# Scalar steps on VectorE, normalising in gated slots on GpSimd, and sums in need order, in a fused attention and GLU kernel

## The chip, the cores and the metric

The kernel runs on one core of a Trainium2 chip. The metric is device time in microseconds (us) of one execution; medians over several executions are quoted. Each execution also has a *span*, the time from the first to the last instruction in the trace, which is some 1.7 us shorter. Five engines work side by side (in the profile before PE is busy for 97% of the span, DVE for 81%), each with its own program: PE (TensorE, matmuls), DVE (VectorE), ACT (ScalarE), POOL (GpSimd) and SP (SyncE, which issues DMAs). The traces show DVE and POOL keeping to the order of their programs. In the kernel before, the inputs of a one-element product on POOL were ready by 102.81 us, but behind the steps in front of it in the program it ran only at 109.00 us. DVE stood idle for 3.94 us for its result, and a sum behind that wait, to whose input ACT had nothing left to add after 105.81 us, started only at 109.31 us.

## The reference

The sum of an input, a linear attention with a learned feature map, and a bilinear GLU, both on the layer norm of the input (2048 tokens, width 512, 32 heads of 16, inner width 1792, bf16):

```python
xn = _layernorm(x)
# attention: q, k, v = heads of xn @ wqkv
phi(q) = concat(softmax(q @ w_phi), softmax(-q @ w_phi)); phi(k) likewise
kv = einsum("bhsf,bhsd->bhfd", phi_k, v);  z = sum of phi_k over s
o  = einsum("bhqf,bhfd->bhqd", phi_q, kv) / (einsum("bhqf,bhf->bhq", phi_q, z) + 1e-6)
A  = o @ wo
# GLU
h = (xn @ w_gate) * (xn @ w_up);  B = h @ w_down
return x + A + B
```

## The kernel before

A list scheduler at build time orders the steps on each engine. Matmuls keep the program's order. The tokens are 16 tiles of 128. In *slot* t of the main loop PE computes k features and v of some tile, two to four GLU units (`up`), and from slot 10 on one or two q features.

- A GLU unit is two groups of matmuls into two PSUM banks; ACT copies one out, and DVE multiplies the other with it (line 817, "the gate product" below). There are two pairs of banks, so PE can start the second group of a unit only when the gate product of two units earlier is done.
- A feature tile goes through ACT (two exponentials), DVE (a sum, line 512), ACT (a reciprocal by logarithm and exponential), POOL (lines 520 and 522, scaling one half). A q tile is then transposed by a DMA.

The end of the kernel multiplies h in fp16, with w_down scaled by a power of two (line 699, after the scale is known) and combined by a Strassen-like scheme (`wd_combine`, line 748; sums of h, line 778). Tiles 0 to 3 were computed before their layer norm was known, so their h must be multiplied by a row `r2`: 14 products on POOL (line 727). The parts that the change touches:

```python
    def norms(lo, n, k):                       # line 670
        ...
        pool(lambda e: e.tensor_copy(out=ssqb[:, lo:lo + n], in_=ssq[:, lo:lo + n]), cols, [("ssqb", lo)], n)
        ...                                    # a matmul, a DVE sum, two ACT steps
    def d_scale():                             # line 690, slot 12
        norms(14, 7, 1)
        power_of_two(swd, scl[:, 18:19], [("rn", 14)], "swd", 4096.0)           # DVE, lines 665, 666
        pool(lambda e: e.tensor_tensor(out=scl[:, 22:23], in0=sh, in1=swd, op=ALU.mult), ["sh", "swd"], ["both"], 1)  # line 693
        dve(lambda e: e.reciprocal(out=scl[:, 23:24], in_=scl[:, 22:23]), ["both"], ["rboth"], 1)                      # line 694
        ...
    def normalise(fts):                        # line 724, called in slots 13 to 16
        sc.prio = 2
        for ft in fts:
            pool(lambda e, ft=ft: e.tensor_tensor(out=hH_v[:, ft, 0:512], in0=hT_v[:, ft, 0:512], in1=r2w,
                                                  op=ALU.mult), [("hT", ft, 0), "r2w", ("x", 14), ("x", 15)],
                 [("hT", ft, 0)], 512)
    # ... cut
    for t in range(NT + 3):                    # the slots
        features("ek", t, 1)                   # ... cut: k features, then units, v, q features
```

The scheduler places the products of `normalise` by its own model of time: in the order it built, they start soon after slot 11 and stand between the features on POOL.

The softmax here doesn't subtract the row's maximum and nothing guards it: scores larger than these inputs give would overflow.

## Time and profile before

| | |
|---|---|
| median time | 221.18 us (3 runs, 220.29 to 221.28) |
| span of the profiled run | 219.1 us |
| busy: PE, DVE, ACT, POOL | 97%, 81%, 58%, 39% |

PE is the limit nearly everywhere, so the question is where it waits. From the page of the profile, the shares of busy time and the rows of 40 slices of 5.5 us (each digit is the busy share in tenths; PEclk is the clock granted to PE):

```profile
PE 211.5 (97%) x1472; PEld 127.2 (58%) x1492; DVE 176.9 (81%) x293; ACT 126.2 (58%) x316; POOL 84.4 (39%) x151
...
PE   7899999999999999999979999999999999999995
...
POOL 3032543424023205508999988040313414330220
PEclk9999999999999999999969999999999999999999
```

One slice stands out, the 21st (109.6 to 115.0 us): PE is at 7 and its clock at 6, and POOL is full around it. The stretches around it show both (columns: stretch, its length, then busy time of PE, weight loads, DVE, ACT, POOL, then granted clock, DMA share and GB/s):

```profile
105.00:109.00 4.00, 4.00 (x20) 1.68 (x18) 0.29 (x1) 0.58 (x3) 4.00 (x6) 1.00 0.10 18
109.00:111.10 2.10, 0.18 (x1) 0.00 (x0) 1.87 (x5) 0.53 (x3) 2.10 (x4) 1.00 0.00 0
111.10:114.70 3.60, 3.54 (x12) 1.36 (x13) 3.60 (x9) 2.12 (x4) 3.60 (x7) 0.53 0.42 81
114.70:120.00 5.30, 5.25 (x31) 2.48 (x30) 5.30 (x8) 3.60 (x10) 5.14 (x7) 1.00 0.29 56
120.00:130.00 10.00, 9.84 (x52) 4.48 (x52) 9.97 (x11) 6.51 (x16) 8.76 (x10) 1.00 0.25 49
```

DVE and ACT stand nearly still from 105 to 109 us, while POOL is full; then PE stands still; then PE works at half clock; and from 111 to 130 us DVE has no idle time left. The timeline shows why (start, length, engine, line; in brackets the idle time before and what ended it):

```profile
104.08 1.21 DVE L512 TENSOR_REDUCE arena<-arena 128x64 f32<-128x1024 bf16 x1
...
105.42 3.40 POOL L727 TENSOR_TENSOR arena<-arena 128x512 f16<-128x512 bf16 x3
108.77 0.27 POOL L520 TENSOR_TENSOR arena<-arena 128x32 f32<-128x32 f32 x1
109.00 0.20 POOL L693 TENSOR_TENSOR arena<-arena 128x1 f32<-128x1 f32 x1
...
109.23 0.16 DVE L694 RECIPROCAL arena<-arena 128x1 f32<-128x1 f32 x1 [3.94 <-POOL arena L693]
109.31 1.20 DVE L512 TENSOR_REDUCE arena<-arena 128x64 f32<-128x1024 bf16 x1
...
110.42 0.68 DVE L817 TENSOR_TENSOR arena<-ps,arena 128x512 f16<-128x512 f32 x1
...
111.16 1.39 PE L244 MATMUL ps<-arena 128*128 128x512 bf16 x3 [1.98 <-DVE arena L665]
```

The one-element product of line 693 stands on POOL behind normalising products. DVE, in its program's order, waits 3.94 us for it, and behind DVE's wait stands the gate product (110.42 us) that PE needs. (PE's wait is put down to line 665, a tiny step that ended at 111.16 us, 0.06 us after the gate product; no matmul reads its result.)

### The profile page before, as it was taken

Reading aid. Unit: us, or ns where it says so; the run is one execution under the profiler, and the core shown is the slowest. Engines: PE = TensorE matmul, PEld = TensorE weight load, DVE = VectorE, ACT = ScalarE, POOL = GpSimd, SP = SyncE. Lnnn points to the kernel's source line nnn. Section 1 sums busy time; section 2 is a strip of 40 time slices with the busy share of each in tenths; the row PEclk is TensorE's granted clock in tenths of the full one; section 3 lists DMA queues with packets and bytes.
Section 4 is the critical chain, followed back from the end, with each engine's and each line's share of the span. In section 5 each row is a group of like instructions: output and inputs, shape, how many; then the busy total and the mean of one; then the engine's idle time right before and its main releaser. Section 6 shows DMA issues by size and latency. Waiting matters only on the chain.

```text
span 219.1 us, 4039 instructions
## 1 busy us (share of the span) xinstructions
PE 211.5 (97%) x1472; PEld 127.2 (58%) x1492; DVE 176.9 (81%) x293; ACT 126.2 (58%) x316; POOL 84.4 (39%) x151
## 2 busy tenths in 40 slices
PE   7899999999999999999979999999999999999995
PEld 2474444444444454444324444455988889899984
DVE  3848999997699898777299998988999999785332
ACT  5558899878778636767256586644343542622330
POOL 3032543424023205508999988040313414330220
PEclk9999999999999999999969999999999999999999
DMA  5999790079400000021233322546053494654431
GB/s 169 288 297 372 182 136 0 15 209 306 99 0 0 0 0 3 0 61 39 49 68 60 65 48 51 96 126 114 2 138 72 130 121 112 158 123 123 104 88 48
DMA packets 49076, 22.30 MB, mean 102 GB/s; under 512 B 38048, under 2 KB 47392, under 8 KB 49056
## 3 DMA queue, kind: packets, MB, share of 16 engines
q1 hardware_dynamic: 48112, 21.39, 41.8%
q10 hardware_dynamic: 944, 0.66, 1.0%
q8 instruction: 11, 0.18, 0.3%
q14 instruction: 9, 0.07, 0.1%
HBM read 11.03 MB, written 2.10 MB: 60 GB/s over the span
## 4 chain that ended last, share of the span: by engine, by line
PE 78%; DVE 6%; issue 5%; POOL 5%; DMA 3%; ACT 1%; SPq 0%; POOLq 0%
PE ps L244 74%; POOL arena L727 3%; DMA arena<-in_A_wqkv_dram 3%; DVE arena L512 3%; PE ps L619 2%; DVE arena L699 2%; DVE arena L817 1%; PE ps L562 1%; POOL arena L522 1%; ACT arena L225 1%; PE ps L374 1%; POOL arena L520 1%; DVE arena L550 0%; SPq L269 0%; DVE arena L842 0%
## 5 line engine op out<-in xcount | busy, mean ns | idle before, releaser
L244 PE MATMUL ps<-arena 128*128 128x512 bf16 (+2 forms) x1156 | 201.6, 330 | 3.8 <-DVE arena L665 2.0
L244 PEld LDWEIGHTS ps<-arena 128*128 128x128 bf16 (+1 forms) x1176 | 112.4, 98 | 78.8 <-DVE arena L665 2.5
L225 ACT ACTIVATE arena<-ps 128x512 bf16<-128x512 f32 (+4 forms) x107 | 53.3, 530 | 37.6 <-PE ps L619 16.5
L225 ACT ACTIVATE arena<-arena 128x32 f32<-128x32 f32 (+7 forms) x117 | 38.8, 345 | 21.3 <-DVE arena L512 18.1
L512 DVE TENSOR_REDUCE arena<-arena 128x64 f32<-128x1024 bf16 x32 | 38.7, 1213 | 8.2 <-ACT arena L225 8.0
L817 DVE TENSOR_TENSOR arena<-ps,arena 128x512 bf16<-128x512 f32 (+1 forms) x56 | 38.0, 683 | 8.2 <-ACT arena L225 4.5
L225 ACT ACTIVATE arena<-ps,arena 128x512 bf16<-128x512 f32 (+1 forms) x49 | 31.0, 653 | 12.2 <-PE ps L244 12.1
L522 POOL TENSOR_TENSOR arena<-arena 128x512 bf16<-128x512 bf16 x32 | 34.5, 1080 | 1.1
L520 POOL TENSOR_TENSOR arena<-arena 128x32 f32<-128x32 f32 x32 | 9.3, 292 | 52.5 <-DVE arena L817 29.6
L862 POOL TENSOR_TENSOR arena<-arena 128x256 f32<-128x256 f32 x16 | 11.0, 711 | 45.6 <-ACT arena L225 45.6
L842 DVE SCALAR_TENSOR_TENSOR arena<-ps,arena 128x256 bf16<-128x256 f32 x32 | 14.9, 479 | 12.1 <-PE ps L244 11.9
L778 DVE TENSOR_TENSOR arena<-arena 128x896 f16<-128x896 f16 x32 | 22.1, 715 | 0.0
L727 POOL TENSOR_TENSOR arena<-arena 128x512 f16<-128x512 bf16 x14 | 17.4, 1255 | 6.7 <-DMA arena<-r2row 6.7
L225 ACT ACTIVATE ps<-ps 128x256 f32<-128x256 f32 x24 | 8.8, 368 | 16.0 <-PE ps L244 15.7
L629 DVE TENSOR_TENSOR arena<-ps,arena 128x512 bf16<-128x512 f32 x16 | 10.9, 685 | 1.6 <-ACT arena L225 1.6
L654 DVE SCALAR_TENSOR_TENSOR arena<-arena 128x1024 bf16<-128x1024 bf16 x7 | 11.9, 1721 | 0.0
L401 DVE BATCH_NORM_STATS2 arena<-arena 128x6 f32<-128x512 bf16 x16 | 10.5, 671 | 0.1
L550 DVE TENSOR_TENSOR arena<-ps,arena 128x512 bf16<-128x512 f32 x14 | 9.5, 682 | 0.0
L562 PEld LDWEIGHTS ps<-arena 128*128 128x128 bf16 x128 | 6.2, 99 | 3.9 <-issue 0.6
L459 POOL TENSOR_SCALAR arena<-arena 128x1 f32<-128x1 f32 x12 | 3.3, 302 | 12.0 <-ACT arena L225 12.0
L562 PE MATMUL ps<-arena 128*128 128x68 bf16 x128 | 6.6, 195 | 0.0
L619 PE MATMUL ps<-arena 128*128 128x68 bf16 x128 | 6.5, 194 | 0.0
(52 smaller groups left out, 72.2 us busy)
## 6 DMA issues: line engine op xcount, KB each, us to landing
arena<-in_A_x_dram SPq DMA_DIRECT2D x9, 256.0 KB, 3.1
out_dram<-arena SPq DMA_DIRECT2D x15, 128.0 KB, 2.0
arena<-in_B_w_down_dram SPq DMA_DIRECT2D x1, 1792.0 KB, 8.2
arena<-in_A_x_dram SPq DMA_DIRECT2D x3, 512.0 KB, 4.2
arena<-arena SPq DMA_TRANSPOSE x44, 3.1
arena<-in_B_w_gate_dram SPq DMA_DIRECT2D x1, 640.0 KB, 8.5
arena<-in_B_w_up_dram SPq DMA_DIRECT2D x1, 640.0 KB, 9.7
arena<-in_B_w_gate_dram SPq DMA_DIRECT2D x1, 512.0 KB, 5.1
```

Of the source, the lines that this page charges most:

```text
L225: return sc.step(ACT, lambda e: e.activation(out=out_ap, in_=in_ap, func=func, scale=scale, **kw), reads, writes, 130.0 + 0.833 * n)
L244: ins = e.matmul(out_ap, lhsT=l, rhs=r, start=start and i == 0, stop=stop and i == npair - 1, **kw)
L512: dve(lambda e: e.tensor_reduce(out=sm, in_=e_v, axis=AX.X, op=ALU.add), [(name, s, 0), (name, s, 1)], [("sums", sr)], 1024)
L520: pool(lambda e: e.tensor_tensor(out=rat, in0=sm[:, :, 0], in1=rs[:, :, 1], op=ALU.mult), [("sums", sr), ("rs", n)], [("rat", n)], 32)
L522: pool(lambda e: e.tensor_tensor(out=e_v[:, :, 1, :], in0=e_v[:, :, 1, :], in1=rat[:, :, None].to_broadcast([128, H, 16]), op=ALU.mult), [ ...
L562: ins = e.matmul(bank(c // 4, (c % 4) * CW, CW), lhsT=ek[:, c * 128:(c + 1) * 128], rhs=vs[:, c * CW:(c + 1) * CW], start=(t == 0 and c % ...
L654: dve(lambda e: e.scalar_tensor_tensor(out=junk, in0=i_ap, scalar=1.0, in1=i_ap, op0=ALU.mult, op1=ALU.mult, accum_out=ssq[:, col:col + 1] ...
L727: pool(lambda e, ft=ft: e.tensor_tensor(out=hH_v[:, ft, 0:512], in0=hT_v[:, ft, 0:512], in1=r2w, op=ALU.mult), [("hT", ft, 0), "r2w", ("x" ...
L778: dve(lambda e, k=k, i0=i0, i1=i1, op=op: e.tensor_tensor(out=s_block(p, k), in0=i0, in1=i1, op=op), ks + more, [s_key(p, k)] + over.get(k ...
L817: dve(lambda e: e.tensor_tensor(out=h_v[:, ft, sg * 512:(sg + 1) * 512], in0=bank(bu), in1=g, op=ALU.mult), [("ps", bu), ("g", s)] + ([("j ...
L842: dve(lambda e: e.scalar_tensor_tensor(out=stg, in0=bank(b, 0, 256), scalar=inv, in1=resid, op0=ALU.mult, op1=ALU.add), [("ps", b), rkey, ...
L862: pool(lambda e, h=h: e.tensor_tensor(out=xs[h], in0=s7, in1=xr_tile(t1)[:, h * 256:(h + 1) * 256], op=ALU.add), ["s7", ("xr", t1 % 4)], [ ...
```

## The change

Its intent: take POOL out of the chain of scale steps; have POOL normalise h of tiles 0 to 3 in slots 11 to 15, three units a slot, each group only after the slot's latest GLU unit is gated, so that the products keep to their slots; and compute the sums of a pair in the order in which the products at the end need them. The diff, cut to its core:

```diff
     def norms(lo, n, k):
-        pool(lambda e: e.tensor_copy(out=ssqb[:, lo:lo + n], ...
+        dve(lambda e: e.tensor_copy(out=ssqb[:, lo:lo + n], ...
     def h_scale():
-        pool(lambda e: e.tensor_tensor(out=scl[:, 20:21], in0=scl[:, 12:13], in1=scl[:, 13:14], op=ALU.mult),
+        dve(lambda e: e.tensor_tensor(out=scl[:, 20:21], in0=scl[:, 12:13], in1=scl[:, 13:14], op=ALU.mult),
     def d_scale():
-        pool(lambda e: e.tensor_tensor(out=scl[:, 22:23], in0=sh, in1=swd, op=ALU.mult), ["sh", "swd"], ["both"], 1)
+        dve(lambda e: e.tensor_tensor(out=scl[:, 22:23], in0=sh, in1=swd, op=ALU.mult), ["sh", "swd"], ["both"], 1)
...          (r2w moves from the space of x tiles 14, 15 to that of 12, 13)
-    def normalise(fts):
+    def normalise(fts, after):
-                   op=ALU.mult), [("hT", ft, 0), "r2w", ("x", 14), ("x", 15)],
+                   op=ALU.mult), [("hT", ft, 0), "r2w", ("x", 12), ("x", 13)] + after,
...          (h_combine: the order of its sums)
-        sc.prio = 2
+        sc.prio = 2 if p else 1
         for k, i0, i1, op, more in ((1, a21, a22, ALU.add, []),
+                                    (3, a11, a21, ALU.subtract, [s_key(p, 1)]),
                                     (2, s_block(p, 1), a11, ALU.subtract, [s_key(p, 1)]),
-                                    (3, a11, a21, ALU.subtract, [s_key(p, 1)]),
                                     (4, a12, s_block(p, 2), ALU.subtract, [s_key(p, 2)])):
...          (row_of_r2 is called in slot 10 instead of 11)
-        if 13 <= t < 17:
-            normalise(range(14 * (t - 13) // 4, 14 * (t - 12) // 4))
+            if 11 <= t < NT:
+                normalise(range(14 * (t - 11) // 5, 14 * (t - 10) // 5), [("hT", *latest[0])])
```

More of the change, by code (lines that the diff above doesn't have):

```diff
@@ L672, in norms @@
         cols = [("ssq", c) for c in range(lo, lo + n)]
-        pool(lambda e: e.tensor_copy(out=ssqb[:, lo:lo + n], in_=ssq[:, lo:lo + n]), cols, [("ssqb", lo)], n)
+        dve(lambda e: e.tensor_copy(out=ssqb[:, lo:lo + n], in_=ssq[:, lo:lo + n]), cols, [("ssqb", lo)], n)
         b = misc_bank()
@@ L719, in row_of_r2 @@
         sc.dma(SP, lambda e: e.dma_start(o, r2s, allow_slow_non_contiguous=True), ["r2s"], ["r2row"], 131072)
-        ks = [("x", 14), ("x", 15)]
+        ks = [("x", 12), ("x", 13)]
         wide = bass.AP(tensor=row.tensor, offset=row.offset, ap=[[0, 128], [1, ND * 128]])
         sc.dma(SP, lambda e: e.dma_start(r2w, wide), ["r2row"], ["r2w"] + ks, 262144, free=ks)
-    def normalise(fts):
+    def normalise(fts, after):
         sc.prio = 2
@@ L732, in _build @@
     r2s = scl[:, 4:4 + ND]
-    r2w = sbf("x", 3584, 512)
+    r2w = sbf("x", 3072, 512)
     tw = {k: sbh(f"tw{k}", 0, NK * 256).rearrange("p (f j) -> p f j", f=NK) for k in (1, 2, 3, 4)}
@@ L978, in scales @@
             h_scale()
+            row_of_r2()
         if 7 <= t < 11:
@@ L981, in scales @@
                 squares("wd", i, last)
-        if t == 11:
-            row_of_r2()
-        elif t == 12:
+        if t == 12:
             d_scale()
```

## The prediction

> **What bounds the kernel now.** TensorE. The page has PE busy 211.5 of 219.1 us (97%), DVE 81%, ACT 58%, POOL 39%. In the stretch table PE is busy in 9.84 to 10.00 us of nearly every 10 us from 20 to 210 us, except around 110 us. In the list of waits PE waited on an engine only once for over 1 us: 1.98 us, from 109.18 to 111.16 us. Right after it (111.1 to 114.7 us) the granted clock is 0.53, and 8 matmuls of 512 columns took 3.52 us, where others take about 0.22 each. The clock record holds half speed for 3.41 us: about 1.7 us more is lost. [...] The stall costs 2.0 + 1.7 = 3.7 us.
>
> **Why PE waits.** The chain of waits runs POOL, DVE, PE. GpSimd waits 6.73 us for the row of r2 (to 99.1 us), then works without a pause: six normalising products (1.1 to 1.2 us each), features, and only at 109.0 us the one-element product of the scales (line 693). DVE, in order, waits 3.94 us for it before the reciprocal (109.23 us). Behind that stand a 1.2 us sum and the gate product that frees the PSUM bank PE wants (ends 111.10 us).
>
> **What the change does.**
> 1. Scalar steps on VectorE: four more DVE instructions of about 0.15 us (the like of lines 665, 666, 694), 0.6 us in all, and the 3.94 us wait gone. Counting from 102.8 us with the trace's durations, the gate product that ended at 111.10 us should end near 107.5, 1.5 us before PE wants its bank; later gates come early enough too. This is the whole gain. The first scale's product and the two copies gain nothing: nothing on PE waited for them.
> 2. Normalising in slots 11 to 15, three per slot: GpSimd's sum is unchanged (14 products, 17.4 us), spread to about 138 us instead of 133.6. Not on PE's path: this h is wanted near 146 us (142 after). The row of r2 keeps its place in the DMA queue, so GpSimd still waits some 6 us for it. Worth 0.
> 3. Sums of the first pair in need order: PE shows no wait from 146 to 160 us. Worth 0.
>
> **Predicted.** 221.18 - 3.7 + 0.1 for added DVE work = 217.6 us, 1.6% faster. Range 216.7 to 219.6. Chances: faster by over 2% 0.06, within 2% 0.92, slower by over 2% 0.02.
>
> **What would show it.** Step 1: no DVE wait at the reciprocal, PE's 2 us wait gone, granted clock 1.00 from 100 to 125 us, about 0.22 us per 512-column matmul there. Step 2: last normalising product near 135 to 140 us; the first sum of the pair doesn't wait for POOL. Step 3: no PE wait in the first output pair. Span near 215.5 us.
>
> **What would make it wrong.** VectorE was full (9.97 of 10 us from 120 to 130 us); with PE earlier, a gate may come late there[...], leaving a gain of 1 to 2 us. GpSimd, in order, may wait for a gated unit and hold features back. The last normalising products may come late for the first sum and stall the start of the outputs. Or the clock drop has a cause other than the wait.

Two passages are cut where marked: one on what brings the half clock, one on how long a wait brings it; no trace of this case shows either. 221.18 - 3.7 + 0.1 = 217.6 us (217.58), with 3.7 = 2.0 (PE's wait of 1.98 us) + 1.7 (3.41 us at half clock), both read from the trace. The "gain of 1 to 2 us" in its last paragraph was the estimate for a half clock that comes back.

## More of the kernel before

The q tiles use a ring of three buffers, so ACT's exponentials of a q tile wait until the DMA has read the tile three before.

- v is computed into a PSUM bank and scaled by DVE (line 550). k, v and q features share two PSUM banks.

## The result

The changed kernel takes 217.51 us (median of 4 runs, 217.38 to 217.83), the kernel before 221.07 us (4 runs, 220.29 to 221.28). The ratio is 0.9847, with a 95% interval of 0.982 to 0.9874. Here and below a ratio is the mean time of one kernel's fast runs over that of the other's in the same rounds, so it is not quite the ratio of the medians. On another occasion the changed kernel took 218.44 us beside 221.80 us, ratio 0.9841 (0.9817 to 0.9865).

The profile after. The page's rows:

```profile
PE 210.7 (97%) x1492; PEld 126.6 (59%) x1492; DVE 178.0 (82%) x297; ACT 126.3 (58%) x316; POOL 82.8 (38%) x147
...
PE   7999999999999999999999979999999999999995
...
POOL 3032453423122023405999699720322413420220
PEclk9999999999999999999999999999999999999999
```

The dip at the 21st slice is gone and the clock is full throughout; a new, smaller dip of PE stands at the 24th (124 to 130 us). The same stretches as before:

```profile
105.00:109.00 4.00, 4.00 (x20) 1.81 (x19) 3.78 (x6) 2.29 (x7) 3.84 (x7) 1.00 0.61 67
109.00:111.10 2.10, 2.10 (x18) 1.11 (x17) 2.10 (x4) 1.17 (x3) 2.10 (x3) 1.00 0.37 68
111.10:114.70 3.60, 3.60 (x19) 1.60 (x18) 3.60 (x5) 2.87 (x9) 3.52 (x5) 1.00 0.48 75
114.70:120.00 5.30, 5.30 (x33) 2.58 (x32) 5.21 (x7) 3.23 (x8) 5.22 (x8) 1.00 0.27 53
120.00:130.00 10.00, 8.90 (x49) 4.00 (x48) 9.62 (x10) 5.83 (x15) 8.21 (x11) 1.00 0.27 52
```

PE now has no idle time until 120 us, and loses 1.10 us in the next 10. The timeline:

```profile
102.65 0.54 DVE L693 TENSOR_TENSOR arena<-arena 128x1 f32<-128x1 f32 x1
...
103.22 0.16 DVE L694 RECIPROCAL arena<-arena 128x1 f32<-128x1 f32 x1
...
105.80 0.68 DVE L817 TENSOR_TENSOR arena<-ps,arena 128x512 f16<-128x512 f32 x1
...
118.48 1.38 DVE L699 TENSOR_SCALAR arena<-arena 128x1024 f16<-128x1024 bf16 x1
...
119.90 1.94 DVE L748 TENSOR_TENSOR arena<-arena 128x1792 f16<-128x1792 f16 x1
...
123.48 1.14 DVE L748 TENSOR_TENSOR arena<-arena 128x1792 f16<-128x1792 f16 x1
...
128.00 0.68 DVE L550 TENSOR_TENSOR arena<-ps,arena 128x512 bf16<-128x512 f32 x1
...
128.73 1.04 PE L244 MATMUL ps<-arena 128*128 128x512 bf16 x4 [1.10 <-DVE arena L550]
```

The reciprocal comes 6 us earlier, without a wait, and the gate product that PE wanted at 109 us ends at 106.5 us. The new wait is for the scaling of v (line 550), which frees a PSUM bank: DVE reaches it late, because it has been busy without a pause and has just combined w_down twice (line 748).

A measure that serves for all runs below: the time on PE from its first state sums (line 562, near 102 us) to its first output heads (line 619, near 145 to 150 us). PE's work in between is the same in every kernel here. It took 46.47 us before and 43.63 us after; the fastest profile of all had 42.36 us. Against that fastest profile PE lost about 4.1 us there before and 1.3 us after. Of the difference of 2.84 us, the wait of 1.98 and the half clock (3.41 us of half speed, so 1.71) went, and 1.10 came: 2.59. The remaining 0.25 us are small gaps that I do not assign.

### The profile page after: what moved, and what is told of

Same layout as the page of the kernel before. It is cut to its first block, busy times and chain, and to the rows that moved or that the text cites. A ratio compares the mean times of both kernels' runs of the same rounds, so it can differ in the third digit from the quotient of the medians.

```text
span 216.1 us, 4056 instructions
## 1 busy us (share of the span) xinstructions
PE 210.7 (97%) x1492; PEld 126.6 (59%) x1492; DVE 178.0 (82%) x297; ACT 126.3 (58%) x316; POOL 82.8 (38%) x147
## 4 chain that ended last, share of the span: by engine, by line
PE 91%; DMA 3%; DVE 3%; issue 1%; ACTq 0%; ACT 0%; DVEq 0%
PE ps L244 86%; DMA arena<-in_B_w_gate_dram 3%; PE ps L619 2%; PE ps L562 2%; DVE arena L512 1%; DVE arena L817 1%; PE ps L374 1%; DVE arena L748 0%; DVE arena L550 0%; DVE arena L842 0%; ACTq L289 0%; ACT L1074 0%; PE ps L480 0%; DVEq L1175 0%
## 5 line engine op out<-in xcount | busy, mean ns | idle before, releaser
L522 POOL TENSOR_TENSOR arena<-arena 128x512 bf16<-128x512 bf16 x32 | 35.4, 1108 | 1.3
L520 POOL TENSOR_TENSOR arena<-arena 128x32 f32<-128x32 f32 x32 | 8.7, 271 | 47.9 <-DVE arena L817 30.5
L778 DVE TENSOR_TENSOR arena<-arena 128x896 f16<-128x896 f16 x32 | 22.7, 727 | 0.1
L461 DVE TENSOR_SCALAR arena<-arena 128x512 bf16<-128x512 bf16 x12 | 5.3, 484 | 1.7 <-DMA arena<-arena 1.4
L619 PE MATMUL ps<-arena 128*128 128x68 bf16 x128 | 6.5, 194 | 0.0
```

The lines of the kernel that those rows point to most:

```text
L522: pool(lambda e: e.tensor_tensor(out=e_v[:, :, 1, :], in0=e_v[:, :, 1, :], in1=rat[:, :, None].to_broadcast([128, H, 16]), op=ALU.mult), [ ...
L619: ins = e.matmul(bank(b0 + c // 4, (c % 4) * CW, CW), lhsT=ph[:, c, :], rhs=kvz_v[:, c, :], start=True, stop=True)
L778: dve(lambda e, k=k, i0=i0, i1=i1, op=op: e.tensor_tensor(out=s_block(p, k), in0=i0, in1=i1, op=op), ks + more, [s_key(p, k)] + over.get(k ...
```

## The experiments

### First call: which part gives the gain

Four kernels on one chip, with 11 runs of the kernel before (median 221.17 us). `s1_only` and `line693_only` start from the kernel before:

```diff
  s1_only: all three lines of step 1 as in the change (two helpers and line 693: pool -> dve)
  line693_only:
-        pool(lambda e: e.tensor_tensor(out=scl[:, 22:23], in0=sh, in1=swd, ...
+        dve(lambda e: e.tensor_tensor(out=scl[:, 22:23], in0=sh, in1=swd, ...
  s2_only: the change with these three lines back on pool, and without step 3
  no_s3: the change without its edit of h_combine
```

> The kernel before with step 1 alone (all three kinds of scalar steps on VectorE). My theory: step 1 by itself takes away DVE's 3.94 us wait and with it PE's 1.98 us wait and the half-rate window, so the time is that of the full change, 217.5 us within 0.4, clock 1.00 from 100 to 125 us. Rival: the full change also needs the moved normalising to be fast; then this run keeps part of the stall and lies at 218.5 to 220.

Measured: 219.77 us (219.45 to 219.89), ratio 0.993 (0.9915 to 0.9944). So step 1 alone gives 1.4 us, not 3.5: my theory fell, and the rival's range of 218.5 to 220 holds it. DVE's wait of 3.94 us and PE's of 1.98 us are gone as expected, and the clock is full; but PE has a new wait. The timeline of this kernel:

```profile
105.62 3.41 POOL L727 TENSOR_TENSOR arena<-arena 128x512 f16<-128x512 bf16 x3
...
109.52 1.11 POOL L522 TENSOR_TENSOR arena<-arena 128x512 bf16<-128x512 bf16 x1
...
114.10 0.60 ACT L225 ACTIVATE arena<-ps 128x512 bf16<-128x512 f32 x1 [4.20 <-DMA arena<-arena]
...
115.36 0.82 PE L244 MATMUL ps<-arena 128*128 128x512 bf16 x3 [1.73 <-ACT arena L225]
```

and its chain of waits:

```profile
105.67 3.36 POOL arena L727 x3
109.04 0.41 POOL arena L520
...
109.52 1.12 POOL arena L522
...
110.70 3.04 DMA arena<-arena
...
114.10 1.21 ACT arena L225 x3
```

Three normalising products (3.4 us) stand on POOL in front of the scaling of a q tile. The q tile's transposition by DMA starts only after that (3.04 us), and ACT, which wants the buffer of that q tile for a new one, waits 4.20 us. Behind ACT, in order, stands what PE needs. This is the path that step 2 is about, and that the prediction left out.

> The kernel before with only the product of the two scales (line 693) moved to VectorE; both copies and the first scale's product stay on GpSimd. My theory: this one instruction is the cause, so the time equals that of step 1 alone, 217.3 to 217.9 us. Rival: the other moved scalar steps carry some of the gain; then it is slower than step 1 alone by 0.5 us or more.

Measured: 219.57 us (219.35 to 220.9), ratio 0.9936 (0.9914 to 0.9957), the same as step 1 alone. The absolute range I gave was that of the fallen theory; the comparison it was made for holds: line 693 is all of step 1's gain, and the copies and the first scale's product give nothing.

> The kernel before with step 2 alone: normalising in slots 11 to 15, all scalar steps still on GpSimd. The prediction gave step 2 no gain: then about 221 us. Rival theory: what counts is only when the product at line 693 runs; here three normalising products instead of six stand before it, so by the durations in the trace it runs near 106 us instead of 109, DVE waits about 1 us instead of 3.9, PE does not wait, no half-rate window: 217.5 to 218.5 us. Then the steps 1 and 2 are two cures of one stall, and their gains do not add.

Measured: 219.75 us (219.47 to 220.71), ratio 0.9941 (0.9921 to 0.996). The prediction's "worth 0" is refuted, and so is the rival that step 2 alone cures all. Line 693 runs at 106.59 us instead of 109.00, DVE waits 1.70 us instead of 3.94, and PE's first wait is gone, as the rival had it. But VectorE then runs late, and PE has two waits of 1.39 and 1.37 us on ACT, which waited for DVE's sums of line 512 (2.72 and 2.81 us). From its timeline:

```profile
106.82 0.16 DVE L694 RECIPROCAL arena<-arena 128x1 f32<-128x1 f32 x1 [1.70 <-POOL arena L693]
...
115.37 6.30 PE L244 MATMUL ps<-arena 128*128 128x512 bf16 x28 [1.39 <-ACT arena L225]
...
125.88 6.22 PE L244 MATMUL ps<-arena 128*128 128x512 bf16 x28 [1.37 <-ACT arena L225]
```

So each step alone gives about 1.4 us and both together 3.4 to 3.6. The product of the two ratios is 0.987; that of the whole change, 0.9847 and 0.9841, is a little lower, with 0.987 inside the first interval and just outside the second. The gains add up, or slightly more. Each step alone does take away PE's first wait, but each leaves other waits behind it (by way of the q buffer in step 1 alone, of DVE's late sums in step 2 alone), and the two together leave less than either. On top of step 1, step 2 is worth about 1.8 us (0.9847 against 0.993).

> The changed kernel without step 3 (the sums of the first pair in the old order, at the lower priority). My theory: PE waits for none of these sums, so 217.5 us within 0.3. Rival: with PE some 3 us earlier the old order makes it wait at the first output pair, 0.5 us or more slower.

Measured: 217.98 us (217.25 to 218.55), ratio 0.9851 (0.983 to 0.9872), which is the ratio of the whole change (the absolute range, 217.5 within 0.3, was missed by 0.2 us; the changed kernel itself was not in this call). Step 3 gives nothing that can be seen here; its profile shows no PE wait at the output pairs either.

### Second call: the mechanisms

On another chip, with 11 runs of the kernel before (median 220.52 us).

The first kernel adds to step 1 alone a fourth q buffer, in space that the output heads use later. The order of instructions on POOL, ACT, SP and PE stays as it was, and on DVE up to 145 us:

```diff
+    q_slot = lambda t: t % 4 if t < 12 else t % 3
-        s = t % (RK if w else RQ)
-        e_v = sb(name, s * 1024, 1024)...
+        s = t % RK if w else q_slot(t)
+        e_v = (sb(name, s * 1024, 1024) if s < 3 or w else sb("o", 0, 1024))...
...          (the same in q_transpose; num_stage of tiles 0, 1 waits for that buffer's last reader)
```

> Step 1 alone, with a fourth buffer for the q features of tiles 3, 7 and 11 (in memory that the output heads use later); order of instructions on GpSimd, ScalarE and the DMA queue unchanged. Step 1 alone was 219.77 us: ScalarE waited 4.2 us for the transposition of an older q tile, PE 1.73 us for ScalarE. Theory A: late normalising on GpSimd holds back the q features, their transposition, and through the ring of three buffers ScalarE; with a fourth buffer that wait goes, PE's 1.73 us too: 217.6 to 218.4 us. Theory B: the loss of step 1 alone is VectorE's backlog[...]; then the buffer changes nothing: 219.4 us or more.

Measured: 218.56 us (218.06 to 218.87), ratio 0.9902 (0.9882 to 0.9922). It is better than step 1 alone (0.993) though not as much as expected. The waits of PE:

```profile
PE ps L244 <- DVE arena L550: 1.3, 1, 1.3
...
PE ps L244 <- DVE arena L817: 0.2, 1, 0.2
```

The wait for ACT (1.7 us) is gone with the buffer, without any instruction moved on POOL: theory A is right about the path. With that wait gone PE comes to 127 us earlier, and there it waits 1.3 us for DVE at line 550, where in step 1 alone it waited 0.17: DVE's backlog, which theory B named, is the next limit behind the first. That is why the time lies above the range. It also takes back most of what the first wait gave: PE leaves line 550 at 129.70 us, against 129.78 in step 1 alone. The rest of the gain comes later, where step 1 alone has a second wait of ACT for a q buffer (3.40 us, to 134.05) and this kernel has none.

The buffer wins back about 0.6 us by the ratios (0.993 to 0.9902), or 1.3 us of the stretch on PE, of the 1.8 or 1.9 us that step 2 adds to step 1. What makes up the rest was not isolated; DVE's combinations of w_down (line 748) take 5.8 us here and 5.25 us in the changed kernel, which is a part of it at most.

The second kernel changes one priority in the changed kernel:

```diff
     def wd_combine(k):
-        sc.prio = 1
+        sc.prio = 2
```

> The changed kernel with the four combinations of w_down at a lower priority in the list scheduler; it moves one of them (1.1 us on VectorE) behind the product for v that PE waited 1.10 us for near 128 us. Theory: that wait goes, 216.2 to 216.8 us. Rival: the work moved later makes another wait of about the same size: 217.3 us or more.

Measured: 216.71 us (216.63 to 216.76), ratio 0.9821 (0.98 to 0.9841). One combination of w_down moves behind line 550 in DVE's order, line 550 starts at 126.30 us instead of 128.00, and the list of PE's waits from 100 to 150 us is empty. The stretch on PE is 42.59 us.

The third gives a wrong result on purpose (relative error 0.16): the 14 normalising products are left out.

```diff
-            if 11 <= t < NT:
+            if 99 <= t < NT:
                 normalise(...)
```

> WRONG RESULT ON PURPOSE: the changed kernel without the 14 normalising products on GpSimd. Theory: while GpSimd normalises, the scalings of w_down (7 on line 699, 6.2 us in all now, about 0.9 each, though the same form on line 709 takes 0.4 to 0.5) and the combinations (1.1 to 1.9 us) on VectorE are slowed; without it line 699 sums to under 4 us, PE's 1.10 us wait near 128 us goes, 216.3 to 216.8 us. Rival: VectorE's durations don't depend on it and the wait stays: 217.3 us or more.

Measured: 216.75 us (216.29 to 217.13), ratio 0.9822 (0.9799 to 0.9845). DVE's order is unchanged and PE's wait is gone. DVE's scalings of w_down, line 699, by their least, median and greatest duration in ns, first in the changed kernel:

```profile
L699 DVE TENSOR_SCALAR arena<-arena x7: 483/773/1380, 107.9 to 118.5; 128x1024 f16<-128x1024 bf16 x7
```

and without the normalising products:

```profile
L699 DVE TENSOR_SCALAR arena<-arena x7: 473/479/620, 108.0 to 117.3; 128x1024 f16<-128x1024 bf16 x7
```

The seven take 6.2 us with GpSimd's products beside them and 3.2 us without (sums of the timeline's lines). The median of the combinations (line 748) hardly moves, 1112 to 1092 ns, but each of the two kernels has at least one of 1.9 us; in the timeline without normalising that one lies at 132 us (1.91 us). The sums (line 512, 1219 ns) and the gate products (line 817, 681 ns, one operand in PSUM) have the same median with and without. Why line 699 is slowed and these are not, the traces do not show. So with the products of GpSimd beside them DVE's scalings took 3.0 us longer (6.2 against 3.2), in a stretch where DVE had no time to give (in the changed kernel it is busy for 8.81 of the 8.90 us from 111.1 to 120 us).

The fourth holds DVE up in the changed kernel:

```diff
-        dve(lambda e: e.tensor_tensor(out=scl[:, 22:23], ...
+        dve(<two tensor_reduce of 1024 columns into unused columns>, then the same tensor_tensor
```

> The changed kernel with two extra sums of 1024 columns (about 1.2 us each) on VectorE in front of the product of the scales. Theory: VectorE has no idle time from 103 to 128 us, so the 2.4 us come out at PE's wait near 128 us (3.5 us instead of 1.1)[...]: 219.9 to 221.8 us, with a half-rate window in the clock record. Rival: there is slack of 2 us or more and the time stays under 218.2 us.

Measured: 220.51 us (220.22 to 220.81), ratio 0.9994 (0.9968 to 1.002). A clause of the expectation is cut: it held a wait of 3.5 us to be long enough for the half clock and added 1.7 us for it, which no trace shows. With that term the sum was 217.5 + 2.4 + 1.7 = 221.6 us, without it 219.9, the low end of the range. The total is in the range, but not for the whole reason given. DVE has no slack here: 2.34 us put in come out as 3.0 us (220.51 against 217.51 us, in different calls), or 2.7 us of the stretch on PE (46.30 against 43.63). PE now has three waits (1.29, 0.43 and 1.29 us) rather than one of 3.5, two of them by way of ACT. They sum to 3.0 us, but 1.1 us of that was there before. The seven scalings of line 699 also got longer by the shift, from 6.2 to 7.1 us. The clock stayed full (1.00 from 100 to 150 us); the half clock was no part of it.

### Third call: the better version again, and the half clock

On the chip of the first call, with 11 runs of the kernel before (median 221.80 us).

> The changed kernel again, unedited, to compare with the other runs of this call on the same chip: 217.2 to 217.9 us.

Measured: 218.44 us (218.16 to 219.17), ratio 0.9841; the absolute range was missed, and the kernel before was slower in this call too (221.80 us).

> The changed kernel with the combinations of w_down at the lower priority, again, beside the changed kernel on the same chip. It was 216.71 us beside 217.51 in another call. Theory: 0.6 to 1.0 us faster than the changed kernel here too. Rival: the difference was between chips; then under 0.3 us.

Measured: 217.45 us (216.66 to 217.79), ratio to the kernel before 0.9789 (0.9763 to 0.9814). Against the changed kernel in the same rounds the means are 217.36 and 218.52 us, a ratio of 0.9947: 1.2 us faster, a little more than expected, so it beats both kernels. (One small wait of PE, 0.20 us for DVE at line 817, is in this profile.)

`s3_only` is the kernel before with the edit of `h_combine` alone; nothing before 140 us differs.

> The kernel before with step 3 alone (order of the sums). Theory: no gain, the time of the kernel before within 0.5 us. If the half clock follows from PE's 2.0 us wait, this run shows both again at 109 to 115 us, since nothing before 140 us is changed; if the half clock was chance, the wait is there without it and the time is some 1.7 us lower in the profiled run.

Measured: 222.17 us (222.08 to 222.44), ratio 1.0004 (0.9972 to 1.0036): no gain. But the profile says something else of interest. PE's waits in this kernel:

```profile
PE ps L244 <- DVE arena L665: 3.3, 1, 3.3
PE ps L244 <- ACT arena L225: 1.6, 2, 0.9
```

and from the timeline, the matmuls after the old wait and after the last new one:

```profile
112.73 1.90 PE L244 MATMUL ps<-arena 128*128 128x512 bf16 x8 [3.28 <-DVE arena L665]
...
128.15 6.22 PE L244 MATMUL ps<-arena 128*128 128x512 bf16 x28 [0.86 <-ACT arena L225]
```

The old wait is there, longer (3.28 us: the row of r2 landed at 100.6 us in this profile, at 99.0 in that of the kernel before), and **no half clock followed it**: the next eight matmuls took 1.90 us, not 3.52. The time was not lower for that. Instead PE waited twice more, 0.76 and 0.86 us, within the next 17 us. That second half of the expectation is refuted.

`before_held1` holds DVE up by one sum in front of the reciprocal of the kernel before:

```diff
-        dve(lambda e: e.reciprocal(out=scl[:, 23:24], ...
+        dve(<one tensor_reduce of 1024 columns>, then the same reciprocal
```

> The kernel before with one extra sum of 1024 columns (1.2 us) on VectorE in front of the reciprocal, so PE's one wait should be 3.1 to 3.2 us instead of 2.0. Theory: again one half-rate window of 3.4 us right after it, and the time is that of the kernel before plus 1.0 to 1.6 us. Rival: no half-rate window; then about the time of the kernel before or less.

Measured: 222.48 us (2 runs), ratio 1.0019 (0.9979 to 1.0059). PE waited 4.03 us and not 3.1 to 3.2 (the row of r2 was late here too), a half-rate window of some 3.4 us followed (a granted clock of 0.83 from 110 to 120 us), and after it PE waited for nothing more (to 160 us). The time rose by 0.4 us by the ratio, which its interval does not tell from none; 1.0 to 1.6 us had been expected. The same matmuls after the wait, here and then in the kernel before, and a later line of the kernel before:

```profile
113.01 3.42 PE L244 MATMUL ps<-arena 128*128 128x512 bf16 x8 [4.03 <-DVE arena L665]
...
111.16 3.52 PE L244 MATMUL ps<-arena 128*128 128x512 bf16 x8 [1.98 <-DVE arena L665]
...
126.58 3.35 PEld L244 LDWEIGHTS ps<-arena 128*128 128x128 bf16 x17 [0.60 <-ACT arena L225]
```

Both runs suggested that a half clock and later waits stand in for each other. The runs of the kernel before bear it out, since each lists its mean clock: 0.992 or less I take as a run with a half-rate window like that of the profile (which lists 0.992), 0.999 or 1.0 as one without (the changed kernel's profile, full until 215.4 us, lists 0.999). (A run whose clock records are missing also lists 1.0, as the profile of `s3_only` does; with the runs of 0.999 alone, the means without the window are 221.00 and 220.47 us.)

| call | with the window | without |
|---|---|---|
| first | 221.37 us (mean of 7) | 221.06 us (mean of 4) |
| second | 221.05 us (mean of 4) | 220.42 us (mean of 7) |
| third | 222.05 us (mean of 10) | 221.92 us (1 run) |

The window takes 1.7 us from PE's speed (3.41 us at 0.50), but a run with it is only 0.1 to 0.6 us longer. Behind PE's wait DVE is full (9.97 of 10 us from 120 to 130 us); in these two profiles a faster PE just arrives at DVE's queue earlier and waits there: counted from the end of PE's long wait, DVE starts its first combination of w_down after 11.56 us with the half clock (`before`, 122.72 us) and after 11.55 us without (`s3_only`, 124.28 us), and PE starts the 61st matmul of 512 columns after 15.42 us in both (126.58 and 128.15 us). The two new waits of `s3_only` are for ACT, which waited 1.63 and 2.30 us for DVE's sums of line 512. In another kernel the window may cost more: the one run of `line693_only` with a mean clock of 0.992 took 220.90 us, the five others 219.35 to 220.06.

What brings the half clock is not shown. In the kernel before it ran from 111.28 to 114.69 us (3.413 us at 0.50), 105.813 us (31 times 3.413) after the clock had last risen. In the changed kernel, which has no such dip, the clock was full for 211.626 us (62 times 3.413) until it fell at the kernel's end, near 215.4 us. In the 3.42 us just before the half clock of the kernel before, PE was busy for 1.44 us, so idle for 58%. The length of the wait alone does not tell: the slow clock followed waits of 1.98 and 4.03 us, but the matmuls after the wait of 3.28 us in `s3_only` were not slow (eight in 1.90 us, against 3.52 in the kernel before). That profile has no clock records. Nor is it shown why 21 of the 33 runs had the window: the waits of runs without a profile are not on record.

All profiles together, by the stretch on PE from the first state sums to the first output heads (the profile is one run, the median and the ratio are of all runs):

| kernel | stretch on PE, us | median time, us | ratio to before |
|---|---|---|---|
| before | 46.47 | 221.07 | 1 |
| step 1 alone | 45.50 | 219.77 | 0.993 |
| step 2 alone | 45.54 | 219.75 | 0.9941 |
| step 1 alone, fourth q buffer | 44.23 | 218.56 | 0.9902 |
| the change | 43.63 | 217.51 | 0.9847 |
| the change, combinations later | 42.59 | 216.71 | 0.9821 |
| the change without normalising (wrong) | 42.36 | 216.75 | 0.9822 |
| line 693 alone | 45.28 | 219.57 | 0.9936 |
| the change without step 3 | 43.81 | 217.98 | 0.9851 |
| the change, DVE held up | 46.30 | 220.51 | 0.9994 |
| third call: the change | 43.88 | 218.44 | 0.9841 |
| third call: the change, combinations later | 42.99 | 217.45 | 0.9789 |
| third call: step 3 alone | 47.78 | 222.17 | 1.0004 |
| third call: before, DVE held up | 48.33 | 222.48 | 1.0019 |

## Why the prediction was right, and where it was not

The time was right (217.6 predicted, 217.51 measured), and so were most of the signs it named. The way to it was right in part only.

- **Which wait is the limit, and that the change removes it.** Right. The wait at the reciprocal, PE's 1.98 us and the half clock are gone. The gate product ends at 106.5 us, an estimate of 107.5 having been given.
- **"The stall costs 2.0 + 1.7 = 3.7 us."** Wrong as an amount that can be won back. The 1.7 us of the half clock were read correctly, but they hid DVE's backlog: runs of the kernel before without the window were only 0.1 to 0.6 us faster. What removing a loss gives depends on the queue behind it.
- **Step 1 "is the whole gain".** Wrong. Alone it gives 1.4 us (0.993). PE then waits 1.73 us for a q buffer, by way of POOL, DMA and ACT, and some more later.
- **Step 2 "not on PE's path ... worth 0".** Wrong; this is the step that failed most clearly. The argument looked at when the normalised h is wanted (late, which was right: the last product ended at 138.0 us, the first sum at 143.26 us did not wait for it). It did not look at what the products hold back behind them in POOL's order: line 693 (at 106.59 us with step 2 alone, 109.00 before) and the scaling of the q tiles. Step 2 alone gives 1.4 us, about 1.8 us on top of step 1, and the change needs both.
- **Step 3 worth 0.** Right: the ratio is 0.9851 without it and 0.9847 with it.
- **"Later gates come early enough too".** Nearly: the gates did, but the scaling of v in the same queue did not, and PE waits 1.10 us near 128 us. The last paragraph had named this risk (a full DVE met by an earlier PE). PE's waits of 1.10 us here and of 1.73 us in step 1 alone were met with a granted clock of 1.00.
- **GpSimd's wait for the row of r2.** Right in kind: 7.34 us, "some 6" having been predicted; the row landed at 99.4 us and normalising started at 99.53. Its small scattered write to DRAM took 8.6 us from issue to landing and the broadcast read of it 4.6 us (8.1 and 4.6 us in the kernel before).

So the total came out by luck, because two errors offset each other: the gain of one stall was put too high, and the gain of the other step at nothing. The total alone would have hidden both; the runs of single steps showed them.

## What to carry to other kernels

When work is moved on an engine that keeps to its program's order, as POOL and DVE did here (6.2 and 3.94 us of waiting behind others' work), ask not only when its own result is wanted but what stands behind it in the queue, and follow that through DMAs and rings of buffers to the bottleneck engine. A wait and the slow clock after it were not the gain here (3.7 us counted, 1.4 us from step 1 alone): look at how full the next engine is behind it, and run each part of a change alone before saying which one paid. Where the bottleneck's feeder is full, an instruction with slack can be moved behind one without: here one combination of weights moved so gave another 1.2 us in the call that compared the two kernels side by side.
